# First hidden group by halves of x and units, a hundred small matmuls on zeros at the start, and more matmul groups by halves

## The chip, the cores and the metric

The kernel runs on one core of one Trainium2 chip. The metric is the device time of one execution in microseconds (us); the time before is the median of three runs.

## The reference

Sliding-window causal attention (8 batches, 8 heads, 576 positions, head width 64, window 64), and then a gated feed-forward layer on its output, for 4608 tokens of width 512 with a hidden width of 1536:

```python
scores = scale * np.matmul(q, k.transpose(0, 1, 3, 2))
mask = (rel >= 0) & (rel < window)              # rel = query - key
attn = softmax(np.where(mask, scores, -1e9))
x = np.matmul(attn, v).transpose(0, 2, 1, 3).reshape(B * S, H * D)
gate = np.maximum(x @ w_gate, 0.0)
val = x @ w_val
return (gate * val @ w_out).astype(np.float32)
```

Inputs and output are float32; the kernel computes its products in float16 with float32 sums.

## The kernel before

**Tokens.** The tokens are cut into tiles: tile 0 has 384 tokens, tile 1 has 192, tile 2 has 448, and the others 512. Attention for the first tokens goes by units of 192 tokens (three windows of 64): units 0 and 1 make tile 0, unit 2 makes tile 1. A unit's attention runs through scores (`u_st`, line 277, four row groups of TensorE side by side), exponentials on ScalarE (`u_exp`, L311), masks on VectorE (for units 0 and 1 a bias product on TensorE instead, `bias_mm`, L244), values (`u_pv`, L348, four column groups side by side), reciprocals of the row sums (`u_recip`, L362), the norm on VectorE (`u_norm`, L369) or ScalarE (`u_norm_act`, L381, six instructions), and a transpose on VectorE (`u_turn`, L391). `hh` is 0 or 1, one half of the heads, which is one half of the 512 channels of x: `u_turn(u, (0,))` gives the channel chunks 0 and 1 of unit u's columns of `xt`, and `u_turn(u, (1,))` the chunks 2 and 3.

**Feed-forward of the first tiles.** The hidden features go in slices of 128 (f, 12 of them; "feature 2" is such a slice), each computed as four matmuls over the four channel chunks c. `first_hidden` does blocks 0 to 3 of tile 0: all products with w_gate (RELU on ScalarE, L677), then all with w_val (product with the gate on VectorE, L683 or L686). It packs the work into four blocks, numbered n, one PSUM bank each: block 0 in bank 0 holds features 0 and 1 of unit 0, bank 1 feature 2 of units 0 and 1, bank 2 feature 3 of both units, and bank 3 features 0 and 1 of unit 1. `STEPS` lists, for w_gate and for w_val, in which order (n, chunks cs, units of the bank us, ends) the products go; the weights' first half (`a` = 0) serves chunks 0 and 1, the second half chunks 2 and 3. Then `hidden(0, ...)` does features 4 to 11 in groups of four (L634); `halves` says how many of a group's first features are done by halves: first chunks 0 and 1 of all of them, then chunks 2 and 3. `hidden(1, ...)` does tile 1, and `output(0, ...)` multiplies the hidden values of tiles 0 and 1 with w_out (`out_mm`, L1145): four groups of 128 tokens, features 0 to 3 of all four groups first, then 4 to 7, then 8 to 11. There, features from `OUT_SPLIT` on (but the last) are done as two matmuls of 256 columns rather than one of 512. All later tiles go through seven-product block multiplications (`fast_hidden` L740, `SevenOut` L966), which the change does not touch.

**Order.** The engines' queues are written in an order fixed by hand: `tc.manual_schedule()` and a small planner, `Weaver`. `W.at(t, fn)` puts work of the other engines at a planned time; `W.clock` counts planned TensorE time; `W.advance` records what is due. What a change of the TensorE order does to the clock can thus move other work between two TensorE instructions. Banks are taken in turn (`one_bank`: banks 0 to 3; `two_banks`: 4 to 7). In the first group, the banks 0 to 3 have just held the values of units 0 (banks 0 and 1) and 1 (banks 2 and 3).

**Weights.** GpSimd issues the weights' transfers (`w_load`, L160 and L162), in the order w_gate 0 to 3, w_val 0 to 3, w_gate 4 to 7, w_val 4 to 7, values of v, w_gate 8 to 11, w_val 8 to 11, each of w_gate and w_val in two transfers (a = 0 and 1). `w_need` keeps the planner from recording a product ahead of the planned landing of its weights.

**Products on zeros.** `zero32` is a cleared piece of a tile (`wts`) that is filled later. `keep_hot` (L241) and `heat` (L238) multiply with it and change no result; `heat(1, ...)` is one matmul of 512 columns, which stands ahead of `first_hidden`'s products.

Of the kernel before, what the change touches and what calls it, by code (L numbers as in the profile page):

```python
# [10 lines left out]
FP32 = mybir.dt.float32  # L11
FP16 = mybir.dt.float16
# [35 lines left out]
def kernel(  # L48
# [10 lines left out]
    nc = tc.nc  # L59
# [7 lines left out]
    NC = DM // 128  # L67
    NF = DF // 128
    G = 4
    scale = 1.0 / float(D) ** 0.5  # L70
    TT = 2 * U
# [17 lines left out]
    singles = [psum.tile([128, 512], FP32, name=f"bank{i}") for i in range(8)]  # L89
# [9 lines left out]
    us = persist.tile([128, 4, 2, 128 * HF], FP16)  # L99
# [33 lines left out]
    def v_fixed(i, eng):  # L133

        eng.memset(v16s[i][:, :, :, D:VW].bitcast(FP32), ONE_ONE)
        eng.memset(v16s[i][0:64, 0].bitcast(FP32), 0.0)
# [6 lines left out]
    units = {}  # L143
# [3 lines left out]
    def xt_tile(t):  # L147
        if t not in xts:
            xts[t] = x_sb.tile([128, NC, WT], FP16, name="xt")
        return xts[t]  # L150
# [1 line left out]

    w_done = {}

    def w_load(wt, src, f0, f1, landed):

        if wt is not wo:
            ns = slice(128 * f0, 128 * f1)
            for a in range(2):
                nc.gpsimd.dma_start(wt[:, 2 * a:2 * a + 2, ns], src.rearrange("(a p e) n -> a p e n", a=2, e=2)[a, :, :, ns])  # L160
        if wt is wo:
            nc.gpsimd.dma_start(wo[:, f0:f1], src.rearrange("(c p) n -> p c n", p=128)[:, f0:f1])  # L162
        w_done.update(((wt.name, f, a), landed - 1.3 * (1 - a)) for f in range(f0, f1) for a in range(2))

    def w_need(wt, f, a=1):
        while (wt.name, f, a) not in w_done:
            W.pop()
        W.advance(w_done[wt.name, f, a])
# [7 lines left out]
    def qk_load(b, name, hh):  # L176

        tile_ = nat[b, name, hh] = nats[:, 2 * "kq".index(name) + hh]
        src = (q if name == "q" else k)[b, G * hh:G * hh + G]
        nc.gpsimd.dma_start(tile_, src.rearrange("h (i j) d -> (h i) (j d)", i=32))  # L180
# [54 lines left out]
    def heat(n, to, start=True):  # L235

        for _ in range(n):
            nc.tensor.matmul(to, zero[:, 0:128], zero[:, 0:to.shape[1]], start=start, stop=start, skip_group_check=not start)  # L238
# [9 lines left out]
    def one_bank():  # L248
        taken["one"] += 1
        to = singles[(taken["one"] - 1) % 4]  # L250
        while id(to) in unread:
            W.pop()
        return to
# [9 lines left out]
    def st_tiles(u):  # L263
        d = units.setdefault(u, {})
        if u == 0:
            d["st"] = [one_bank() for _ in range(G)]
        else:
            halves = [two_banks() for _ in range(2)]
            d["st"] = halves[0] + halves[1]
        part_written(d["st"])  # L270
        d["p"] = [None] * G
# [57 lines left out]
    def u_pv(u, hhs=(0, 1), banks=None):  # L329

        d = units[u]
        if "pv" not in d:
            if u >= 6:
                d["pv"] = [bank() for _ in range(2)]
                unread.update(map(id, d["pv"]))
            elif banks:
                d["pv"] = [one_bank() for _ in range(2)]
            else:
                d["pv"] = two_banks()
            part_written(d["pv"])  # L340
        for hh in hhs:
            to = d["pv"][hh]
            for w in range(UB):
                b, vw = divmod(UB * u + w, NG)
                for s in range(2):
                    for j in range(G):
                        c = VW * (2 * w + s)
                        nc.tensor.matmul(  # L348
                            to[32 * j:32 * j + 32, c:c + D + 1], p_of(u, G * hh + j, w)[:, 32 * s:32 * s + 32],
                            v16s[b % 2][:, vw, G * hh + j, 0:D + 1],  # L350
                            start=True, stop=True, skip_group_check=True)
        return 0.27 * len(hhs)
# [66 lines left out]
    def part_written(banks):  # L419
        written.update((id(to), 0) for to in banks)  # L420
# [225 lines left out]
    def first_hidden():  # L646

        g_sb, done = gs[0] = g_sb_p.tile([128, NF, WT], FP16, name="g_sb"), {}
        xt = xt_tile(0)
        r2s = [f_sb.tile([128, 2, WT], FP32, name="pr", bufs=4) for _ in range(2)]  # L650
        r_sbs = [r2s[n // 2][:, n % 2, 0:TT] for n in range(4)]
        blocks = (((0, 0), (1, 0)), ((2, 0), (2, 1)), ((3, 0), (3, 1)), ((0, 1), (1, 1)))
        parts = lambda tile: tile.rearrange("p (w n) -> p w n", w=2)
        STEPS = (
            ((0, (0, 1), (0, 1), False), (0, (2, 3), (0, 1), True), (1, (0, 1), (0, 1), False), (2, (0, 1), (0, 1), False), (1, (2, 3), (0, 1), True), (2, (2, 3), (0, 1), True), (3, (0, 1, 2, 3), (0, 1), True)),
            ((0, (0, 1), (0, 1), False), (2, (0, 1), (0, 1), False), (0, (2, 3), (0, 1), True), (2, (2, 3), (0, 1), True), (3, (0, 1, 2, 3), (0, 1), True), (1, (0, 1, 2, 3), (0, 1), True)),
        )

        def products(h, i, n, cs, us=(0, 1), more=False):
            wt = (wg, wv)[i]  # L660
            block = blocks[n]
            W.advance(W.clock)
            w_need(wt, block[-1][0], cs[-1] // 2)
            whole = i == 0 and n in (1, 2)
            for c in cs if whole else ():
                f = block[0][0]
                nc.tensor.matmul(h[:, 0:TT], wt[:, c, f * 128:f * 128 + 128], xt[:, c, 0:TT],  # L667
                                 start=(c == 0), stop=(c == NC - 1), skip_group_check=True)
            for m in () if whole else us:
                f, u = block[m]  # L670
                for c in cs:
                    nc.tensor.matmul(h[:, U * m:U * m + U], wt[:, c, f * 128:f * 128 + 128], xt[:, c, U * u:U * u + U],  # L672
                                     start=(c == 0 and m == us[0] and not more), stop=(c == NC - 1), skip_group_check=True)
            W.clock += len(us) * len(cs) * (U + 7) / 2400.0

        def relu(n, h):
            nc.scalar.activation(r_sbs[n], h[:, 0:TT], ACT.Relu)  # L677

        def gate(n, h):
            (f, u), (f1, u1) = blocks[n]  # L680
            if f == f1:
                to = g_sb[:, f:f + 1, 0:TT]
                nc.vector.tensor_tensor(to, r_sbs[n].rearrange("p (w n) -> p w n", w=1), h[:, 0:TT].rearrange("p (w n) -> p w n", w=1), MUL)  # L683
                done[f] = TT
            else:
                nc.vector.tensor_tensor(g_sb[:, f:f + 2, U * u:U * u + U], parts(r_sbs[n]), parts(h[:, 0:TT]), MUL)  # L686
                done.update({f: U * u + U, f1: U * u + U})

        for i, then in enumerate((relu, gate)):
            hs = {}  # L690
            for n, cs, us, ends in STEPS[i]:
                more = n in hs
                if not more:
                    hs[n] = one_bank()
                    part_written([hs[n]])
                products(hs[n], i, n, cs, us, more and 0 not in us)
                if ends:
                    W.at(W.clock, lambda n=n, h=hs[n], then=then: then(n, h))
# [186 lines left out]
    wts = persist.tile([128, 4, HF, QN], FP16)  # L885
# [296 lines left out]

    LAST = len(widths) - 1
    BY_ACT = ()
    SPLIT, OUT_SPLIT = [(i, f) for i in range(2) for f in range(4, NF)], 7
    HALVED = [(4, 0, 'P5')] + [(4, 1, name) for name in ('P1', 'P2', 'P3', 'P4')]
    FAST_OUT = (LAST - 5, LAST - 4, LAST - 3, LAST - 2, LAST - 1, LAST)
    O_SUMS = {2: [(24.0, 2, (1, 1)), (26.0, 0, (0, 1))], 3: [(8.0, 3, (1, 0)), (34.0, 1, 2), (34.1, 3, 0)]}
# [8 lines left out]
    with tc.manual_schedule():  # L1197
# [4 lines left out]
            first_load(name)  # L1202
        for name in "kq":
            qk_load(0, name, 1)
        warm = consts.tile([128, 2], FP32)
        nc.vector.memset(warm, 0.0)
        nc.scalar.activation(warm[:, 1:2], warm[:, 0:1], ACT.Exp)
        for i in range(2):
            v_fixed(i, nc.vector)
        zero32 = wts.rearrange("p a f n -> p (a f n)").bitcast(FP32)[:, 0:384]  # L1210
        nc.vector.memset(zero32, 0.0)
        zero = zero32.bitcast(FP16)
        st_tiles(0)
        bands()
        v_load(0, ((1, 0, 128), (3, 0, 64)))
        v_load(1, ((3, 64, 128), (5, 0, 128)))
        w_load(*G3[0], 15.2)
        w_load(*V3[0], 17.7)
        k_zeros()
        band_bias()  # L1220
# [25 lines left out]
        u_turn(0, (0,))  # L1246
        for hh in range(2):
            u_pv(1, (hh,), True)
        heat(1, units[1]["st"][3])
        for hh in range(2):  # L1250
            u_recip(1, (hh,))
        u_norm_act(1, 1)
# [108 lines left out]

        W.advance(15.3)
        first_hidden()
        hidden(0, ((0, TT),), 4, NF, 4, split=SPLIT, halves={(8, 0): 4, (8, 1): 3})
        hidden(1, ((0, U),), each=4, banks=[0, 1, 4, 5, 2, 3, 0, 1, 2, 3, 0, 1])
        taken["one"] += 2
        output(0, (0, 1, 2, 3), (0, 4, 8, NF))
# [71 lines left out]
```

## Time and profile before

| | us |
|---|---|
| median of 3 runs | 298.24 (298.19 to 298.33) |
| the profiled execution | 298.17 |
| its span | 296.5 |
| around the span | 1.67 |
| TensorE matmul busy | 286.9 (97%) |
| TensorE weight loads busy | 241.8 (82%) |
| VectorE busy | 255.4 (86%) |
| ScalarE busy | 203.5 (69%) |
| GpSimd busy | 190.2 (64%) |
| first TensorE matmul starts | 4.42 |
| first product with w_gate starts | 13.80 |

The span is the time between the first and the last instruction of the profiled execution. "PE" is TensorE's matmuls and "PEld" its weight loads, "DVE" is VectorE, "ACT" ScalarE, "POOL" GpSimd and "SP" SyncE. [...] Times given below as "at 13.57" are us from the start of the span.

### The profile page before, as it was taken

How to read it: one execution, taken by the hardware profiler on the slowest of the kernel's cores; microseconds unless marked ns; L12 is line 12 of the kernel's file. 1: busy time of each engine (PE TensorE's matmuls, PEld its weight loads, DVE VectorE, ACT ScalarE, POOL GpSimd, SP SyncE). 2: the span in 40 equal slices, each digit the busy share in tenths (PEclk: the TensorE clock that was granted, in tenths of full speed). 3: DMA queues.
4: the chain of work that ended last, by engine and by line, in shares of the span. 5: the costliest groups of instructions: out<-in, count | busy, mean ns of one | idle time of the engine just before them, and what ended most of it. 6: DMA issues, size and time to landing. Idle time of an engine off the chain costs nothing.

```text
span 296.5 us, 11064 instructions
## 1 busy us (share of the span) xinstructions
PE 286.9 (97%) x4659; PEld 241.8 (82%) x4659; DVE 255.4 (86%) x513; ACT 203.5 (69%) x409; POOL 190.2 (64%) x217
## 2 busy tenths in 40 slices
PE   4799999999999999999999999999999999999995
PEld 2489966996588657998888888888888888888894
DVE  5988989888889799999999999999858985896585
ACT  3744367888288849983897489857985798538860
POOL 8767667898918628476948594859275617441751
PEclk9999999999999999999999999999999999999999
DMA  7999999987998689911599149913911210021013
GB/s 217 185 197 202 195 194 200 237 102 145 156 211 160 103 140 168 212 51 38 85 219 120 42 69 219 127 48 70 172 24 38 75 38 0 3 95 51 1 39 106
DMA packets 62610, 35.22 MB, mean 119 GB/s; under 512 B 39648, under 2 KB 56672, under 8 KB 62560
## 3 DMA queue, kind: packets, MB, share of 16 engines
q0 software_dynamic: 49376, 20.26, 57.9%
q1 hardware_dynamic: 12752, 13.93, 15.2%
q8 instruction: 36, 0.59, 0.8%
q10 hardware_dynamic: 432, 0.33, 0.3%
q14 instruction: 14, 0.11, 0.1%
HBM read 37.75 MB, written 9.44 MB: 159 GB/s over the span
## 4 chain that ended last, share of the span: by engine, by line
PE 94%; DVE 3%; DMA 1%; ACT 0%; issue 0%; DVEq 0%
PE bank L740 49%; PE bank L966 19%; PE bank L874 7%; PE bank L634 6%; PE bank L277 4%; PE bank L1145 4%; PE bank L493 3%; DMA vs<-in_k_dram 1%; PE bank L672 1%; DVE qT L200 1%; DVE kT L200 1%; PE bank L348 1%; PE bank L667 0%; PE bank L241 0%; ACT nats L193 0%; DVE pr L1133 0%
## 5 line engine op out<-in xcount | busy, mean ns | idle before, releaser
L765 POOL TENSOR_TENSOR g_sb<-pr 128x512 f16<-128x512 f32 (+1 forms) x36 | 46.3, 1288 | 50.0 <-ACT pr L782 46.5
L776 DVE TENSOR_TENSOR pr<-bank,pr 128x512 f32<-128x512 f32 (+1 forms) x96 | 60.8, 673 | 4.1 <-ACT pr L759 2.2
L759 ACT COPY pr<-bank 128x512 f32<-128x512 f32 (+1 forms) x96 | 51.1, 588 | 13.8 <-PE bank L740 13.4
L765 DVE TENSOR_TENSOR g_sb<-r,bank 128x512 f16<-128x512 f32 (+1 forms) x48 | 32.4, 676 | 20.1 <-ACT r L809 18.0
L966 PEld LDWEIGHTS <-g_sb 128*128 128x128 f16 x444 | 41.8, 98 | 5.0
L740 PE MATMUL bank<-xc,us 128*128 128x256 f16 (+2 forms) x292 | 42.7, 269 | 0.0
L740 PE MATMUL bank<-xc,vs 128*128 128x256 f16 (+2 forms) x292 | 42.7, 269 | 0.0
L206 POOL DMA_DIRECT2D v<-in_v_dram x41 | 36.8, 1114 | 6.9 <-DMA nats<-in_q_dram 1.5
L740 PEld LDWEIGHTS <-vs 128*128 128x128 f16 x392 | 37.7, 98 | 3.8
L740 PEld LDWEIGHTS <-us 128*128 128x128 f16 x392 | 37.6, 98 | 3.7
L782 ACT ACTIVATE pr<-pr 128x512 f32<-128x512 f32 (+1 forms) x48 | 30.3, 632 | 8.4 <-DVE pr L776 8.4
L450 ACT ACTIVATE pw<-bank 128x512 f16<-128x512 f32 x60 | 32.0, 606 | 2.0 <-PE bank L277 1.6
L809 ACT ACTIVATE r<-bank 128x512 f32<-128x512 f32 (+1 forms) x48 | 28.8, 600 | 5.1 <-PE bank L740 4.1
L740 PEld LDWEIGHTS <-wg 128*128 128x128 f16 x300 | 28.4, 98 | 3.1
L740 PEld LDWEIGHTS <-wv 128*128 128x128 f16 x300 | 28.4, 98 | 2.7
L740 PE MATMUL bank<-xt,wg 128*128 128x256 f16 (+2 forms) x200 | 28.5, 267 | 0.0
L740 PE MATMUL bank<-xt,wv 128*128 128x256 f16 (+2 forms) x200 | 28.5, 267 | 0.0
L916 POOL TENSOR_TENSOR g_sb<-g_sb,xus 128x512 f16<-128x512 f16 x24 | 27.1, 1147 | 0.0
L966 PE MATMUL bank<-wo,g_sb 128*128 128x256 f16 (+1 forms) x222 | 26.6, 270 | 0.0
L749 ACT COPY bank<-bank 128x512 f32<-128x512 f32 (+1 forms) x48 | 25.6, 576 | 0.0
L966 PE MATMUL bank<-wts,g_sb 128*128 128x256 f16 (+1 forms) x222 | 25.6, 270 | 0.0
L459 DVE TENSOR_TENSOR pw<-pw,mask 128x512 f16<-128x512 f16 x60 | 23.2, 429 | 2.2 <-ACT pw L450 1.7
(125 smaller groups left out, 519.5 us busy)
## 6 DMA issues: line engine op xcount, KB each, us to landing
out_dram<-o_sb SPq DMA_DIRECT2D x31, 256.0 KB, 4.0
nats<-in_k_dram POOLq DMA_DIRECT2D x15, 288.0 KB, 5.9
nats<-in_q_dram POOLq DMA_DIRECT2D x15, 288.0 KB, 7.0
v<-in_v_dram POOLq DMA_DIRECT2D x31, 128.0 KB, 8.6
v<-v SPq DMA_DIRECT2D x12, 132.0 KB, 3.4
v<-v SPq DMA_DIRECT2D x24, 66.0 KB, 2.6
wg<-in_moe_w_gate_dram POOLq DMA_DIRECT2D x6, 256.0 KB, 6.8
wv<-in_moe_w_val_dram POOLq DMA_DIRECT2D x6, 256.0 KB, 8.4
```

The lines of the kernel that those rows point to most:

```text
L206: nc.gpsimd.dma_start(v16s[b % 2][lo:hi, g, :, 0:64], v[b, :, 64 * g - 64 + lo:64 * g - 64 + hi].rearrange("h p d -> p h d"))
L450: nc.scalar.activation(d["p"][g].rearrange("p n c -> p (n c)"), d["st"][g], ACT.Exp, scale=scale)
L459: nc.vector.tensor_tensor(d["p"][g], d["p"][g], mask[:, None, :].to_broadcast([128, 2 * QW, 64]), MUL)
L740: nc.tensor.matmul(to[:, HT * m + lo:HT * m + lo + step], w[:, k, 128 * m:128 * m + 128], x[:, k, lo:lo + step], start=(first and m == 0 a ...
L749: nc.scalar.copy(at[j, "B", i][:, 0:TW], at[j, "A", i][:, 0:TW])
L759: nc.scalar.copy(pr[:, i], at[j, "A", i][:, 0:TW])
L765: eng.tensor_tensor(gh[:, f:f + 2, h], pair(r), pair(v), MUL)
L776: nc.vector.tensor_tensor(pr[:, i], to[:, 0:TW], pr[:, i], ADD)
L782: nc.scalar.activation(pr[:, 0], pr[:, 0], ACT.Relu)
L809: nc.scalar.activation(r, to[:, 0:TW], ACT.Relu)
L916: eng.tensor_tensor(to, x, y, op)
L966: nc.tensor.matmul(at[key][:, QN * m * whole:QN * m * whole + n1 - n0], A[:, 128 * m:128 * m + 128], B[:, c, n0:n1] if len(B.shape) == 3 e ...
```

## The change

It has five parts. (1) `STEPS` has a new order for w_gate: eight matmuls on unit 0's first channels (banks 0, 1, 2), then one heating matmul (the entry `None`), then eight on unit 0's second channels, and then unit 1, with bank 3 by halves too; the products of 384 columns (`whole`) are gone, and the heating matmul that stood ahead of the group with them. For w_val, three banks' first halves go first, and bank 1 is last and whole as before. (2) The clearing of `zero32` becomes VectorE's first instruction, and 100 matmuls of 32 x 64 on it, over four column groups in turn, become TensorE's first work. (3) `halves` gets the groups of features 4 to 7: their first two features go by halves. (4) `OUT_SPLIT` goes from 7 to 2. (5) `w_load` gets an argument `parts`, whose default is the old behaviour and which no call gives.

In the recorded queues, ScalarE, GpSimd and SyncE have the same instructions in the same order. On VectorE the clearing stands first, and one mask product of unit 2 passes one gate product (L609). On TensorE, beside the parts named, the 48 value products of unit 2 stand behind the first four matmuls of features 8 to 11 instead of ahead of them.

```diff
-    def w_load(wt, src, f0, f1, landed):
+    def w_load(wt, src, f0, f1, landed, parts=(1, 1)):
...
-            ns = slice(128 * f0, 128 * f1)
-            for a in range(2):
+            for a, n, m in ((a, n, parts[a]) for a in range(2) for n in range(parts[a])):
+                ns = slice(128 * f0 + 512 // m * n, 128 * f0 + 512 // m * (n + 1))
...
         STEPS = (
-            ((0, (0, 1), (0, 1), False), (0, (2, 3), (0, 1), True), (1, (0, 1), (0, 1), False), (2, (0, 1), (0, 1), False), (1, (2, 3), (0, 1), True), (2, (2, 3), (0, 1), True), (3, (0, 1, 2, 3), (0, 1), True)),
-            ((0, (0, 1), (0, 1), False), (2, (0, 1), (0, 1), False), (0, (2, 3), (0, 1), True), (2, (2, 3), (0, 1), True), (3, (0, 1, 2, 3), (0, 1), True), (1, (0, 1, 2, 3), (0, 1), True)),
+            ((0, (0, 1), (0, 1), False), (1, (0, 1), (0,), False), (2, (0, 1), (0,), False), None,
+             (0, (2, 3), (0, 1), True), (1, (2, 3), (0,), False), (2, (2, 3), (0,), False),
+             (1, (0, 1), (1,), False), (2, (0, 1), (1,), False), (3, (0, 1), (0, 1), False),
+             (1, (2, 3), (1,), True), (2, (2, 3), (1,), True), (3, (2, 3), (0, 1), True)),
+            ((0, (0, 1), (0, 1), False), (2, (0, 1), (0, 1), False), (3, (0, 1), (0, 1), False), (0, (2, 3), (0, 1), True), (2, (2, 3), (0, 1), True), (3, (2, 3), (0, 1), True), (1, (0, 1, 2, 3), (0, 1), True)),
         )
...
-            whole = i == 0 and n in (1, 2)
-            for c in cs if whole else ():
-                f = block[0][0]
-                nc.tensor.matmul(h[:, 0:TT], wt[:, c, f * 128:f * 128 + 128], xt[:, c, 0:TT],
-                                 start=(c == 0), stop=(c == NC - 1), skip_group_check=True)
-            for m in () if whole else us:
+            for m in us:
...
+                if step is None:
+                    heat(1, singles[7])
+                    continue
...
-    SPLIT, OUT_SPLIT = [(i, f) for i in range(2) for f in range(4, NF)], 7
+    SPLIT, OUT_SPLIT = [(i, f) for i in range(2) for f in range(4, NF)], 2
...
+        zero32 = wts.rearrange("p a f n -> p (a f n)").bitcast(FP32)[:, 0:384]
+        nc.vector.memset(zero32, 0.0)
+        zero = zero32.bitcast(FP16)
+        for i in range(100):
+            nc.tensor.matmul(singles[7][32 * (i % 4):32 * (i % 4) + 32, 0:64], zero[:, 0:32], zero[:, 0:64], start=True, stop=True, skip_group_check=True)
         warm = consts.tile([128, 2], FP32)
...
-        zero32 = wts.rearrange("p a f n -> p (a f n)").bitcast(FP32)[:, 0:384]
-        nc.vector.memset(zero32, 0.0)
-        zero = zero32.bitcast(FP16)
...
-        heat(1, units[1]["st"][3])
...
-        hidden(0, ((0, TT),), 4, NF, 4, split=SPLIT, halves={(8, 0): 4, (8, 1): 3})
+        hidden(0, ((0, TT),), 4, NF, 4, split=SPLIT, halves={(4, 0): 2, (4, 1): 2, (8, 0): 4, (8, 1): 3})
```

More of the change, by code (lines that the diff above doesn't have):

```diff
@@ L690, in first_hidden @@
             hs = {}
-            for n, cs, us, ends in STEPS[i]:
+            for step in STEPS[i]:
+                if step is None:
+                    heat(1, singles[7])
+                    continue
+                n, cs, us, ends = step
                 more = n in hs
```

## The prediction

> **What bounds the kernel now.** I read the page first, for its chain of work that ended last:
>
> ```profile
> PE 94%; DVE 3%; DMA 1%; ACT 0%; issue 0%; DVEq 0%
> ```
>
> TensorE alone carries 94% of the span, so the question is where the other 6% lie. The waits of PE between 13 and 60 us hold one row, and between 60 us and the end none:
>
> ```profile
> PE bank L672 <- DVE xt L391: 0.7, 1, 0.7
> ```
>
> So after its last stop PE issues without a gap to the end, and whatever ends that stop earlier moves everything behind it. The timeline of PE shows the front (start, busy us, instructions, in brackets the idle time before):
>
> ```profile
> 4.42 2.72 PE L244 MATMUL bank<-bias,ident 128*128 128x384 f16 x8 [4.42 <-DVE bias L130]
> 6.93 1.43 PE L241 MATMUL bank<-wts 128*128 128x384 f32 x2
> 8.35 0.55 PE L277 MATMUL bank<-qT,kT 32*128 32x64 f16 x48
> ...
> 13.09 0.56 PE L348 MATMUL bank<-v,p 128*32 128x65 f16 x48
> 13.57 0.39 PE L238 MATMUL bank<-wts 128*128 128x512 f16 x1
> 13.80 0.49 PE L672 MATMUL bank<-xt,wg 128*128 128x192 f16 x4
> 15.03 0.49 PE L672 MATMUL bank<-xt,wg 128*128 128x192 f16 x4 [0.74 <-DVE xt L391]
> 15.49 1.47 PE L667 MATMUL bank<-xt,wg 128*128 128x384 f16 x8
> 16.80 0.82 PE L672 MATMUL bank<-xt,wg 128*128 128x192 f16 x8
> 17.46 2.80 PE L672 MATMUL bank<-xt,wv 128*128 128x192 f16 x32
> 20.10 2.14 PE L634 MATMUL bank<-xt,wg 128*128 128x192 f16 x24
> ```
>
> A matmul's busy time runs on past the start of the next, so I take costs from starts. 17.46 to 20.10 is 32 matmuls of 192 columns, 0.0825 us each. 15.49 to 16.80 is 8 of 384, 0.164 each. The four at 15.03 need 0.33, so 15.49 comes 0.13 late: a second, hidden wait, for the next transpose. Who ends both is in the timelines of VectorE and ScalarE:
>
> ```profile
> 13.98 0.52 DVE L369 TENSOR_TENSOR xus<-bank,r 128x384 f16<-128x384 f32 x1
> 14.41 1.64 DVE L391 STREAM_TRANSPOSE xt<-xus 128x384 f16<-128x384 f16 x3
> ```
>
> ```profile
> 12.71 2.72 ACT L381 ACTIVATE xus<-bank,r 128x64 f16<-128x64 f32 x12
> ```
>
> The three transposes end at about 14.98, 15.44 and 16.05 (unit 0's second half of channels, then unit 1's two halves), and PE follows each 0.05 later. Before 8.35 PE waits as well: the chain has VectorE's casts and transposes from 5.39 to 10.47, not PE.
>
> **The change, part by part.**
>
> *First group.* Before 15.03 only unit 0's first channels exist, and the old order has four matmuls for them. The new one has eight: blocks 0, 1 and 2. They write banks 0, 1 and 2, which the attention values have just left. Bank 1 is read by the first six of the twelve ScalarE rows, to 14.05; bank 2 by the VectorE row at 13.98, to 14.50. With the heating matmul before them gone, block 0 runs 13.57 to 13.90, block 1 waits to 14.10 and ends at 14.27, block 2 waits to 14.55 and ends at 14.71. The heating matmul, now behind them, takes 0.22 (13.57 to 13.80 in the rows) and ends at 14.93, 0.10 before the transpose lets PE go on at 15.03. That wait itself does not move: its transpose hangs on VectorE's queue, which is the same up to there (and the weights for what follows it land at 14.6, so they would be next, not much earlier).
> Behind 15.03 the old order had 4 of 192, the 0.13, 8 of 384, 8 of 192: 0.33 + 0.13 + 1.31 + 0.66 = 2.43, to 17.46. The new has 24 of 192, ordered so that unit 1's first matmul comes after eight of them, at 15.69 (its transpose: 15.44), and its second channels at 16.35 (16.05). So 24 x 0.0825 = 1.98, to 17.01: **0.45 us earlier**. The split of 384 into two of 192 is within that sum (8 x 0.001).
>
> *What could be late next.* ScalarE's four RELUs free the banks for w_val; they come 0.39 apart, the second at about 16.72, so bank 2 is free by 17.6 and wanted at 17.67; cover 0.07. The w_val steps put three blocks' first halves ahead of the second halves, so w_val's second half is wanted at 18.0 as before. The weights are the transfers that PE now meets 0.45 earlier; issue and landing, one row of the DMA issues for each window around one issue:
>
> ```profile
> wg<-in_moe_w_gate_dram POOLq DMA_DIRECT2D x1, 256.0 KB, 7.1
> ```
>
> ```profile
> wg<-in_moe_w_gate_dram POOLq DMA_DIRECT2D x1, 256.0 KB, 8.7
> ```
>
> The first is w_gate features 4 to 7, second half: issued 12.95, landed 20.07. PE enters that group at 19.65; feature by feature it would want it at 19.98 and stall 0.1. The new grouping (first halves of two features together) wants it at 20.31: no stall, and that is what those two entries are worth. The w_val one delays nothing (landed 23.05, wanted 23.5). The second row is features 8 to 11, first half: issued 16.70, landed 25.35 to 25.4. Here the recorded order moves: the 48 value products of unit 2 now come behind four of these matmuls, not before them, so they are wanted at 25.51 and no longer at 26.56; cover 0.1, and the smallest left. w_out's first third lands at 39.66 (29.46 + 10.2; wanted 40.03), its second at 43.9 (wanted 44.1). On VectorE only one mask product passes one gate product. I price all this at 0, with up to 0.2 in the range.
>
> *Output by halves.* 5 features x 4 row groups: 20 matmuls of 512 become 40 of 256. In rows of one form, 13 of 512 take 2.98 us, the last 0.38 in all: 0.217 each; 8 of 256 take 1.04, the last 0.27: 0.110 each. 20 x (0.220 - 0.217) = **+0.05** (0 to 0.1), all on PE's path.
>
> *Hundred small matmuls.* They start when VectorE's memset, now its first (0.38 us from 0.89), is done: 1.3. Bias products can start at 4.42 at the earliest, since they wait for VectorE. The nearest row is L348, same 32-column weights, 65 columns wide: 13.09 to 13.57 is 48, 10 ns each, four side by side. But the clock is low there in the front: 4.42 to 6.93 is 8 of 384 columns, 0.314 each against 0.164 later (the page's granted clock reads 1.00 all the same). So 20 ns each, 2 us, over at 3.3. The upper bound takes no two side by side: 64/384 of 0.314 is 52 ns, 5.2 us, over at 6.5. I take 2 us, free behind the 4.42. What they may buy is a warm clock under the bias products: 8 x 0.15 = 1.2 us of PE, none of it on the chain, because 8.35 is set by VectorE. **0**. VectorE's reordered memsets end at 2.7 as before and it then idles 1.48: 0. The new argument of the weight load is passed by no call: 0.
>
> *Sum.* -0.45 + 0.05 = -0.40. The profiled execution is 296.5 of span and 1.67 around it, 298.17, 0.07 under the median of 298.24. From the median: 297.84.
>
> **The rivals.**
> *Weights become the wait.* PE runs into features 8 to 11, or w_out, and stands there. For it: cover of 0.1 to 0.2 where there was 0.5 and more. Against: each landing would have to be late by more than that, and transfers in this stretch are issued by POOL without regard to PE. Price: 0.1 to 0.4 given back, 297.95 to 298.25.
> *A faster front.* If the early clock also shortened the chain to 13.57, the gain passes 0.6. Against: the attention products at 8.35 and 10.51 both take 0.55, so the clock was up at 8.35 already. It would take 0.2 us from a chain in which PE's own part is some 2 us: 297.4 to 297.6.
> *Small matmuls outlast the front (slower).* If each costs e ns, they end at 1.3 + 0.1e. By then the clock is up, so bias and keep-hot products take 8 x 0.164 + 0.85 = 2.2, and scores start at 3.5 + 0.1e instead of 8.35. ScalarE has 0.46 us of slack between the two halves of its exponentials; the rest lands on the end. So the loss is 0.1e - 5.3: it begins at e = 53, just past the upper bound above, uses up the gain at 57, and makes 298.8 at 63 and 300.5 at 80. Against: 10 ns in the row at 13.09. For: these would be the first instructions of the queue, a place of which the trace has no row.
> [...]
> *It does not do it.* If block 2's bank came free 0.1 later, the heating matmul would push past 15.03 by as much; it costs 0.1 for each 0.1, down to no gain, 298.2.
>
> **How the numbers follow.** Forecast 0.66 (297.7 to 297.95); weights or the bank 0.14; faster front 0.11; slower 0.09. A measurement of this kernel tells about 0.2%, 0.6 us, from no change. The forecast and the second case lie within it, as do small ends of the others: same 0.78, faster 0.13, slower 0.09. The range takes the faster front down to 297.5 and the weights up, with a little of the slower case, to 298.35.
>
> **What would show it.** In the changed profile: eight products from 13.57, the only PE wait still ending at 15.03 on L391 but under 0.2 long; w_val starting at 17.01 and features 4 to 7 at 19.65; no PE wait behind; the small matmuls over before 4.42 and scores still at 8.35; every later stage earlier by 0.4. It is wrong if 15.03 moves, if a weight load waits at 25.4, or if bias products start after 4.42.

## The result, and the profile after

| | before | after |
|---|---|---|
| median, us | 298.3 (298.19 to 298.98, 12 runs) | 299.88 (299.42 to 302.36, 12 runs) |
| profiled execution, us | 298.17 | 299.65 |
| its span, us | 296.5 | 297.9 |

The ratio of the mean times is 1.0066, with a 95% interval of 1.0046 to 1.0085 (that of the medians is 1.0053). The changed kernel is slower by 0.66%, where a gain of 0.4 us had been forecast.

The timeline of PE in the changed kernel, up to the second pass of features 4 to 7 (start, busy us, instructions, in brackets the idle time before):

```profile
1.40 1.52 PE L1211 MATMUL bank<-wts 128*32 128x64 f16 x100 [1.40 <-DVE warm L1213]
4.40 2.72 PE L244 MATMUL bank<-bias,ident 128*128 128x384 f16 x8 [1.48 <-DVE bias L130]
...
9.05 0.55 PE L277 MATMUL bank<-qT,kT 32*128 32x64 f16 x48 [0.69 <-DVE qT L200]
...
14.28 1.30 PE L670 MATMUL bank<-xt,wg 128*128 128x192 f16 x8
15.42 0.38 PE L238 MATMUL bank<-wts 128*128 128x512 f16 x1
15.74 2.14 PE L670 MATMUL bank<-xt,wg 128*128 128x192 f16 x24
17.71 1.48 PE L670 MATMUL bank<-xt,wv 128*128 128x192 f16 x16
```

The hundred small matmuls are over at 2.92, and the first group runs without a wait: from the first scores (L277) to the first product with w_val it takes 17.71 - 9.05 = 8.66 us, where it took 17.46 - 8.35 = 9.11. That is the gain of 0.45 that was forecast. But the scores themselves start 0.70 later. Among the waits of PE over the whole span, two rows name what else is new (us in total, times, longest):

```profile
PE bank L1147 <- issue: 0.6, 1, 0.6
...
PE bank L634 <- DVE g_sb L609: 0.2, 1, 0.2
```

Both are later than the first group, where the kernel before had no wait at all. Placed in the timeline of PE:

```profile
23.59 2.80 PE L634 MATMUL bank<-xt,wv 128*128 128x192 f16 x32
26.61 0.49 PE L634 MATMUL bank<-xt,wg 128*128 128x192 f16 x4 [0.22 <-DVE g_sb L609]
...
47.92 4.54 PE L1147 MATMUL bank<-wo,g_sb 128*128 128x256 f16 x38
53.03 1.25 PE L1147 MATMUL bank<-wo,g_sb 128*128 128x512 f16 x8 [0.57 <-issue]
```

The span's change is then made up as follows, each from starts on PE (the 0.05 is what is left of the output stage without the stop):

| stage | change, us |
|---|---|
| front, to the first scores (8.35 to 9.05) | +0.70 |
| first group (9.11 to 8.66) | -0.45 |
| w_val of features 4 to 7 to w_val of features 8 to 11 (5.87 to 6.25) | +0.38 |
| forty half-size output products | +0.05 |
| the stop at 53.03 | +0.74 |
| sum | +1.42 (span: 297.9 - 296.5 = 1.4) |

The stop stands at 0.57 in the timeline, because idle time is counted from a matmul's end; between starts the gap is 0.84, of which a product takes 0.11. "issue" says that PE waited for nothing that the profile shows. What stands ahead of the stop in time is among the trace's transfers, on a queue that the page calls "instruction" (packets, MB, share):

```profile
q8 instruction: 37, 0.61, 0.8%
```

The kernel before has this row for it:

```profile
q8 instruction: 36, 0.59, 0.8%
```

0.61 MB in 37 packets is 16 KB each, and one takes 0.88 to 1.6 us. TensorE has 9582 instructions in the changed kernel (4787 matmuls, as many weight loads, and eight of its sequencer) and 9326 before, exactly 256 fewer, and one packet fewer. Of the sixteen kernels profiled here, those with up to 9382 instructions have 36 packets and those with 9442 and more have 37. From these counts I take 256 instructions to a packet: an estimate, since no record says what a packet holds. Counting TensorE's instructions from one in order of their starts, number 1986 is the one that starts late at 53.03. It is 194 + 7 x 256. Below, a block is the 256 instructions from such a number on, and its packet the one as far along in the order of packets, the first with the block at 450; that pairing is mine too. From 15 us on, and leaving out the waits for a tensor that the matmul itself reads or for a bank that it writes, the sixteen kernels have 21 stops of 0.41 to 2.83 us from start to start. **Each of the 21 stands at 194 plus a multiple of 256**, and each ended 1.20 to 1.55 us after the end of a packet. The packet here ran from 50.52 to 51.48, 1.55 us ahead of 53.03; it began 3.5 us after the block before had begun to run (46.98).

The same look at the kernel before shows what the forecast had missed: its instruction 450 = 194 + 256 is the first of the eight last products of w_gate, it starts at 16.80, and the packet ends at 15.22, 1.58 us ahead. The stops ended 1.20 to 1.55 us behind theirs, so by these distances, an estimate, the first group already ran with hardly any cover, 0.03 to 0.38 us.

### The profile page after: what moved, and what is told of

Same layout as the page of the kernel before. It is cut to its first block, busy times and chain, and to the rows that moved or that the text cites. A ratio compares the mean times of both kernels' runs of the same rounds, so it can differ in the third digit from the quotient of the medians.

```text
span 297.9 us, 11320 instructions
## 1 busy us (share of the span) xinstructions
PE 289.0 (97%) x4787; PEld 245.7 (82%) x4787; DVE 256.0 (86%) x513; ACT 203.0 (68%) x409; POOL 189.7 (64%) x217
## 4 chain that ended last, share of the span: by engine, by line
PE 93%; DVE 4%; DMA 1%; issue 0%; ACT 0%; DVEq 0%
PE bank L742 49%; PE bank L968 19%; PE bank L876 7%; PE bank L634 5%; PE bank L1147 4%; PE bank L277 4%; PE bank L493 3%; PE bank L670 2%; DMA vs<-in_k_dram 1%; DVE p L318 1%; DVE qT L200 1%; DVE kT L200 1%; PE bank L348 1%; DVE nats L193 0%; PE bank L241 0%
```

## The experiments

I first ran the parts alone, then moved the blocks, then took parts away from the changed kernel one by one. "Before" had medians of 298.35 to 298.4 in these runs.

**The four parts alone.** Only the new orders (part 1):

```diff
-            ((0, (0, 1), (0, 1), False), (0, (2, 3), (0, 1), True), ...
+            ((0, (0, 1), (0, 1), False), (1, (0, 1), (0,), False), (2, (0, 1), (0,), False), None, ...
```

> Before, with the new order of the first hidden group alone (heating matmul behind the eight products, no other part). Both theories say that this part does what the prediction said: products with w_val start 0.45 us earlier than before, scores still at 8.35, no new wait; span about 296.05 and 297.85 us, with a granted clock of 1.0. If the lower clock of some executions of the changed kernel comes from the heating matmul's new place, some executions here show it too (mean clock 0.992 to 0.998) and are 0.5 to 3 us longer.

298.79, ratio 1.0012 (1.0 to 1.0023): no gain. The timeline of PE shows why:

```profile
13.56 1.30 PE L670 MATMUL bank<-xt,wg 128*128 128x192 f16 x8
14.70 0.38 PE L238 MATMUL bank<-wts 128*128 128x512 f16 x1
15.02 0.82 PE L670 MATMUL bank<-xt,wg 128*128 128x192 f16 x8
16.75 1.48 PE L670 MATMUL bank<-xt,wg 128*128 128x192 f16 x16 [0.92 <-DVE us L561]
```

The eight early products and 15.02 are as forecast, but after eight of the 24 products PE stands until 16.75 (a stop of 1.08, the 0.08 of the product before it not counted), and w_val starts at 18.07. The releaser named (L561 writes `us`, which the first group does not read) is only the event nearest in time: the instruction at 16.75 is number 450, and its packet ran from 14.48.

Only the clearing and the hundred small matmuls (part 2):

```diff
+        for i in range(100):
+            nc.tensor.matmul(singles[7][32 * (i % 4):32 * (i % 4) + 32, 0:64], zero[:, 0:32], zero[:, 0:64], ...
```

> Before, with the clearing first and the 100 small matmuls alone. Theory 1 (each part has a cost of its own): the small matmuls cost something in the front or in the clock: the first load of k lands at 5.2 and not at 4.65, scores at 9.05, span 297.1, and some executions have a mean clock of 0.992 to 0.998 with 0.5 to 3 us more. No stall in the output product. Theory 2 (the late load was chance, and the small matmuls hurt only by shifting the instruction stream by 200): scores at 8.35 in most executions, clock 1.0, and any loss is a gap of TensorE without a wait, somewhere in the output product of tile 0 (0.3 to 0.8 us). If they cost nothing: 298.2.

300.47 (six runs), ratio 1.0063 (1.0039 to 1.0088). The scores start at 8.96, so the late front comes with this part. A stop of 0.72 stands at 230.62, instruction 7874 = 194 + 30 x 256.

Only the output by halves (part 4):

```diff
-    SPLIT, OUT_SPLIT = [(i, f) for i in range(2) for f in range(4, NF)], 7
+    SPLIT, OUT_SPLIT = [(i, f) for i in range(2) for f in range(4, NF)], 2
```

> Before, with OUT_SPLIT 2 alone. Theory 1 (TensorE ran out of instructions at 53.03, since half-size products use up instructions twice as fast behind the 112 small value products): there is a gap without a wait in the output product here too, of 0.4 to 2.4 us by where the fetch falls; span 296.9 to 299. Theory 2 (the 200 added instructions put the fetch there): no gap, +0.05 us, 298.3.

300.6 (six runs), ratio 1.0073 (1.0047 to 1.0098), from 20 more matmuls. Its timeline of PE in the output:

```profile
46.81 0.61 PE L493 MATMUL bank<-v,pw 128*32 128x65 f16 x43
47.35 2.14 PE L1145 MATMUL bank<-wo,g_sb 128*128 128x256 f16 x18
50.62 2.56 PE L1145 MATMUL bank<-wo,g_sb 128*128 128x256 f16 x20 [1.13 <-issue]
```

Instruction 1730 stands at 50.62 after a gap of 1.40; a second gap of 1.35, which I had not expected, is at 114.23, instruction 3778. Each of the two blocks before these numbers holds a run of small value products (L493, 112 from 46.24, of which the first row shows the last 43, and 128 from 108.44), 10 ns from start to start. Ahead of 50.62 the half-size products come at 0.11 us each, where a whole one takes 0.22, so that the count runs twice as fast; at 114.23, far behind the changed output, only the count has moved: this place is number 3738 in the kernel before.

Only the groups of features 4 to 7 by halves (part 3):

```diff
-        hidden(0, ((0, TT),), 4, NF, 4, split=SPLIT, halves={(8, 0): 4, (8, 1): 3})
+        hidden(0, ((0, TT),), 4, NF, 4, split=SPLIT, halves={(4, 0): 2, (4, 1): 2, (8, 0): 4, (8, 1): 3})
```

> Before, with the entries (4, 0) and (4, 1) of halves alone. Theory 1 (recording the four mask products of unit 2 ahead of the first gate product makes TensorE wait for bank 0 at the first product of features 8 to 11): a wait of 0.1 to 0.4 us on L609 near 26, span 296.6 to 296.9, 298.3 to 298.6. Theory 2 (that wait appears only because TensorE came 0.45 us earlier relative to the weights and copies): no wait, 298.2.

298.56, ratio 1.0 (0.9988 to 1.0011): no difference shown. The four mask products of unit 2 stand ahead of the first gate product here too, but PE has no wait on L609: from w_val of features 4 to 7 to w_val of features 8 to 11 it takes 29.70 - 23.83 = 5.87, as before. Theory 2 held.

**Blocks of instructions put to the test.** Sixteen small matmuls (32 instructions) put into idle time of the kernel before, behind the first `keep_hot` product:

```diff
+        for i in range(16):
+            nc.tensor.matmul(singles[7][32 * (i % 4):32 * (i % 4) + 32, 384:448], zero[:, 0:32], zero[:, 0:64], ...
```

> Before, with 16 of the same small matmuls on zeros put behind the first keep-hot product, where TensorE waits for scores until 8.35 anyway; nothing else changes. Theory F (TensorE's instructions come in blocks of 256; the block that begins at its 450th matmul-or-weight-load row is fetched only when the block before it is begun, near 10.7, and is usable at about 16.7; more rows ahead of a fixed point of the program bring that point nearer to the end of what is loaded): scores stay at 8.35, but TensorE stops without a wait at the 450th row, now 16 products earlier in the program, until about 16.7; the first product with w_val starts at 18.9 to 19.2 instead of 17.46 and the span is 1.3 to 1.8 us longer, 297.8 to 298.3 (time 299.5 to 300). Theory Z (what the small matmuls cost, they cost in the front by themselves): no gap, at most 0.1 us, 298.3.

304.5 (four runs), ratio 1.0207 (1.0181 to 1.0233), worse than expected. Timeline of PE:

```profile
13.66 0.39 PE L238 MATMUL bank<-wts 128*128 128x512 f16 x1
16.50 1.44 PE L672 MATMUL bank<-xt,wg 128*128 128x192 f16 x8 [2.45 <-DVE us L561]
17.73 2.43 PE L667 MATMUL bank<-xt,wg 128*128 128x384 f16 x8
```

Number 450 is now the first product with w_gate, and it starts at 16.50, where number 450 ran at 16.80 in the kernel before, so that nearly the whole group lies behind it. After the stop 8 matmuls of 384 columns take 2.27 from start to start, 1.31 before (this execution's mean granted clock is 0.994), and two more stops follow, 0.62 and 1.53 at numbers 1730 and 3778. The scores start at 8.67, 0.32 late. All of that is in the loss of 6 us.

The new orders with eight instructions fewer ahead of the group (the heating matmul out, three float32 products made single float16 ones):

```diff
-        keep_hot(units[1]["st"][3][:, 0:2 * U])
+        heat(1, units[1]["st"][3][:, 0:2 * U], False)
```

> The new first group alone, with 8 rows fewer ahead of it: its own heating matmul is left out and the three float32 keep-hot products are single float16 ones (they change no result). Theory F: the 450th row lies 4 products later in the program, so the 1.08 us gap that the new group alone showed at 16.75 becomes about 0.75, and the span 296.7 to 296.8 (298.4 to 298.5); if the float32 products count as one row pair in the stream, 0.16 to 0.25 instead of 0.33 is saved. Rival (the gap at 16.75 is a wait for VectorE's us products, as the waits have it): gap unchanged at 0.9 to 1.1.

The stop moved four products on, still ending at 16.77, and is 0.83 long now, counted the same way (0.75 expected); w_val started at 17.76, 0.31 earlier than in the run with the new orders alone. The waits name "issue" for it this time, no longer L561. The span stayed at 297.1, at a mean granted clock of 0.994 in this execution. The median is 298.69, ratio 1.0012 (1.0002 to 1.0021).

**One part taken away from the changed kernel.** Without the small matmuls (`for i in range(100)` and its body out):

> The changed kernel without the 100 small matmuls (the clearing stays first). Theory F: scores back at 8.35, but without the 200 rows the 450th row falls into the first group again: a gap of about 1.0 us without a wait near 16.7, and a second one of 0.5 to 2 us behind the 112 value products, where the block that begins at row 1730 is due at about 49; span 297.8 to 299.5, 299.5 to 301. Theory Z (the small matmuls are what costs): no gap near 16.7, span 296.5 to 297.0, 298.2 to 298.7.

302.02 (four runs), ratio 1.0141 (1.01 to 1.0181): 2 us slower than with them. The scores are at 8.34 again, but numbers 450, 1730 and 3778 stop PE, by 1.17, 1.69 and 2.02 us from start to start. In the changed kernel the 200 added instructions move all these places, and one stop of 0.74 is left.

Without the output by halves (`OUT_SPLIT` back at 7):

> The changed kernel with OUT_SPLIT back at 7 (40 rows fewer between 41 and 54 us). Theory F: no gap at 53; front late by 0.6 as in both kernels with the small matmuls, first group 0.45 better, 0.3 to 0.4 lost near 26.6 where the first product of features 8 to 11 waits for a gate product behind four masks: span 296.9 to 297.2, 298.6 to 298.9. Rival (the gap at 53 belongs to something else, a late transfer): gap stays, 299.5.

300.9 (299.14 to 304.27, eight runs), ratio 1.009 (1.0048 to 1.0132). No stop at 53, but one of 0.44 at number 7874, and in the profiled execution, at a mean granted clock of 0.993, the second group of scores takes 0.83 us and not 0.55. The loss at the first product of features 8 to 11, which I had expected to stay, is gone (5.87). No gain over the changed kernel is shown.

Without the two new entries of `halves`:

> The changed kernel without the entries (4, 0) and (4, 1) in halves. Theory M (these entries and the earlier products make the order fixed by hand put four mask products ahead of the gate product that frees bank 0, which costs 0.38 us at 26.61): if the entries are the cause, the wait at 26.61 is gone and the span is 297.5; a wait for the weights of features 4 to 7 of at most 0.1 may come at about 20.7. If the earlier products alone shift the order, the wait stays and the span is 297.9. The stop at 53 stays in both.

299.66, ratio 1.0058 (1.0033 to 1.0083). Timeline of PE:

```profile
23.75 2.80 PE L634 MATMUL bank<-xt,wv 128*128 128x192 f16 x32
26.48 0.56 PE L348 MATMUL bank<-v,p 128*32 128x65 f16 x48
26.97 2.81 PE L634 MATMUL bank<-xt,wg 128*128 128x192 f16 x32
29.62 2.80 PE L634 MATMUL bank<-xt,wv 128*128 128x192 f16 x32
```

The wait is gone: from w_val to w_val 29.62 - 23.75 = 5.87, as before, where the changed kernel has 6.25. But the entries alone do not bring it: it is missing in the run with them alone (above), and in the changed kernel without small matmuls, without the output by halves and with 112 small matmuls the stage takes 5.87 too, with 30 it takes 5.92, though all of these have the entries. With 92 it is there (6.26). The timelines of VectorE and of GpSimd in the changed kernel:

```profile
23.56 2.54 DVE L318 TENSOR_TENSOR p<-p,mask 128x384 f16<-128x384 f16 x4 [0.71 <-ACT p L311]
26.02 1.94 DVE L609 TENSOR_TENSOR g_sb<-pr,bank 128x384 f16<-128x384 f32 x4
```

```profile
23.90 1.72 POOL L216 COPY v<-v 64x512 f16<-64x512 f16 x2 [2.88 <-DMA v<-in_v_dram]
```

The same with the entries alone:

```profile
23.80 2.08 DVE L318 TENSOR_TENSOR p<-p,mask 128x384 f16<-128x384 f16 x4 [0.86 <-ACT p L311]
25.81 1.94 DVE L609 TENSOR_TENSOR g_sb<-pr,bank 128x384 f16<-128x384 f32 x4
```

```profile
23.42 1.72 POOL L216 COPY v<-v 64x512 f16<-64x512 f16 x2 [2.50 <-DMA v<-in_v_dram]
```

All four mask products of unit 2 run ahead of the first gate product, which frees the bank that the matmul at 26.61 writes. They are not of one length: 0.36, 0.77, 1.19 and 0.35 in the changed kernel, the two long ones begun during GpSimd's two copies of v (L216). In the sixteen profiles all 23 mask products of this unit that begin well inside these copies take 0.43 to 1.19, and the 38 others 0.34 to 0.36. In the changed kernel the copies end at 25.61, and the gate product starts 2.43 after PE's w_val (23.59); with the entries alone the copies come earlier, end at 25.14, and it starts 1.98 after (23.83). So the 0.38 needs both, the order of VectorE and masks stretched during the copies. Stretched masks cost without the entries too: the run with small matmuls alone takes 6.09 for this stage and the first trimmed one 6.16, with three masks ahead of the gate product. In the kernel before the gate product runs ahead of the fourth mask product:

```profile
24.65 0.54 DVE L609 TENSOR_TENSOR g_sb<-pr,bank 128x384 f16<-128x384 f32 x1
25.12 0.72 DVE L318 TENSOR_TENSOR p<-p,mask 128x384 f16<-128x384 f16 x1
```

Taking the entries out saved no time in total: the front came at 9.22 in that execution, and PE was idle for 0.9 at 53.10 (1.14 from start to start).

**The number of small matmuls.** 92 and 112 instead of 100 move all blocks by 16 and 24 instructions, and the bias products behind them start at 4.40 and 4.41:

```diff
-        for i in range(100):
+        for i in range(92):
```

> The changed kernel with 92 small matmuls on zeros instead of 100. Theory F (TensorE's instructions come in blocks of 256, counted over matmuls and weight loads, and a block that is begun too early finds nothing): 16 instructions fewer put the block that begins at 53.03 eight output products later, where about 53.2 is wanted and the block is there at about 52.8. So the stop of 0.74 at 53.03 is gone, no other comes, and the profiled span is 0.7 shorter than that of the changed kernel, 297.2 (median about 299.1). Theory P (the stop belongs to the place, the output products by halves): stop stays, span 297.9.

> The changed kernel with 112 small matmuls on zeros instead of 100. Theory F: 24 instructions more put the block's beginning on instruction 1962 of the changed kernel, which runs at 50.88 there; the block is asked for at most 0.1 us earlier, so it is there at about 52.9, and the stop is 1.8 to 2.0 us at about 51 instead of 0.74 at 53.03: span 298.9 to 299.2, median about 301. The twelve matmuls themselves cost nothing, since TensorE waits to 4.40 behind them. Theory P: span 297.9.

With 92 the output runs through, in the timeline of PE:

```profile
48.65 5.62 PE L1147 MATMUL bank<-wo,g_sb 128*128 128x256 f16 x46
54.11 0.55 PE L742 MATMUL bank<-xt,wg 128*128 128x224 f16 x4
```

All 46 products follow each other, and no other stop appears. The span was 297.9 all the same, since the profiled execution ran its attention products slower (0.83 us a group of scores, not 0.55; the mean granted clock is 0.998) and reached w_val at 18.44 instead of 17.71. The median is 299.41 (298.66 to 303.04). The fastest run is 0.76 under the fastest of the changed kernel (299.42), but the fastest without the entries of `halves` (298.87) and with 112 small matmuls (298.88) lie nearly as low with a stop each, so a saving in time is not shown; that the stop is gone is.

With 112 my expectation failed: instruction 1986 ran at 51.49 without a stop, and its packet began at 49.19, 1.7 us after the block before it was begun and not 3.5. A stop came elsewhere, at number 4034:

```profile
113.32 1.68 PE L876 MATMUL bank<-wo,g_sb 128*128 128x512 f16 x7
115.91 1.24 PE L876 MATMUL bank<-wo,g_sb 128*128 128x512 f16 x5 [0.90 <-issue]
```

There the packet began at 113.73, 4.3 us after the block before it was begun (109.41). So in the sixteen kernels the stops stood at counted places alone, but not at all of them, and at the 21 stops the packet began from 0.9 us ahead of the beginning of the block before to 4.3 us behind it. What sets that is open. The reasons that the theories give, a block that is asked for when the one before it is begun, and finds nothing when it is begun too early, are in no record of a trace; what the runs show is the numbers and the times. Over the sixteen profiles the median is 3.25 us behind for packets begun between 13 and 30 us and 0.15 for those after 200 us; the kernel before moves 204 GB/s in its first 60 us and 55 after 200. The median is 299.81 (298.88 to 302.1).

> The changed kernel with 30 small matmuls on zeros instead of 100. It asks what makes the front late (scores at 9.05 instead of 8.35). Theory E (the early fetch of a second block, at 6.55 in the changed kernel, which 100 matmuls bring forward, disturbs the first loads): with 30 the second block is begun only in the attention products, and the scores start at 8.35 again. Theory Q (any work of TensorE ahead of the loads does it, or the clearing): scores still at 8.9 to 9.1. By theory F the third block would then begin where the first group's products stand (instruction 590 of the changed kernel), so a stop of 2 to 3 us between 13.4 and 16.5 and another of about 1 at 47.5 to 49; span 299 to 300.5.

With 30 small matmuls: 307.9, ratio 1.0315 (1.03 to 1.033). Theory E fell: no packet runs early any more (the first is at 13.30), yet the scores still start at 9.06. As theory F says, number 450 now stops PE inside the value products (0.9 idle at 15.75, where 2 to 3 had been expected); there are six stops in all, 7.05 us from start to start, more than I expected, and behind the one at 118.62 the granted clock is 0.5 for 3.4 us (the execution's mean is 0.994). The waits of PE from 60 us on hold two of the six and no other wait:

```profile
PE bank L277 <- issue: 1.7, 1, 1.7
PE bank L493 <- issue: 1.7, 1, 1.7
```

**What is left of the front, and of the first group.** The kernel before with a single small matmul at the start:

> The kernel before with the clearing first and one single small matmul on zeros as TensorE's first work. In the six runs with small matmuls (30 to 112 of them) one 4.6 KB packet of the first loads, begun at 2.11 to 2.17, took 1.0 to 1.5 us, where the longest took 0.45 to 0.77 in the eight runs without; the first k load then landed at 4.9 to 5.35 instead of 4.5 to 4.65. Theory G (TensorE's first instruction, at 1.40 instead of 4.42, sets off something that occupies one transfer engine for about 0.9 us, the length of a packet of instructions): one matmul is enough; one packet begun at about 2.15 takes over 1.0 us, the k load lands at 4.9 to 5.3 and the scores start at 8.9 to 9.1; span 297.0 to 297.4. Theory H (it is the number of matmuls, or their traffic): k load at 4.5 to 4.65 and scores at 8.35, span 296.5 to 296.8.

298.32, ratio 1.0003 (0.9994 to 1.0012), scores at 8.37: theory G fell too. One is not enough, thirty are.

The new orders with none of the `heat` and `keep_hot` products, 14 instructions fewer than the new orders alone:

> The new order of the first group alone, without its heating matmul and without the three products that keep the clock up. Theory F: six instructions fewer than in the run that had three single matmuls there move the block's beginning three products on, to 15 products after the second stop; it is there at about 16.8 still, so the products with w_val start at 17.5 instead of 17.76, about where they start in the kernel before (17.46): span 296.6 to 296.8. Rival: without those products the clock falls to half in the front, scores or attention values take twice their time, and the span is over 297.5.

298.47, ratio 1.0008 (0.9997 to 1.002), span 296.5. Timeline of PE:

```profile
8.44 0.83 PE L277 MATMUL bank<-qT,kT 32*128 32x64 f16 x48 [1.31 <-DVE qT L200]
...
13.61 4.05 PE L670 MATMUL bank<-xt,wg 128*128 128x192 f16 x32
17.50 2.80 PE L670 MATMUL bank<-xt,wv 128*128 128x192 f16 x32
```

w_val starts at 17.50, as theory F said, although the products before it ran slower (32 in 3.89, 0.122 each and not 0.0825), and number 450 stands at 16.76. In the kernel before and in six variants (the new orders alone, both trimmed ones, the changed kernel without small matmuls, the output alone, one small matmul) number 194 runs between 10.76 and 11.09, and number 450 at 16.75 to 16.80, whatever product it is. In these seven kernels no product of the first group that stands behind number 450 ran before 16.75. The time itself is not fixed: with sixteen added matmuls number 450 runs at 16.50, and with 30 small matmuls at 15.75, its packet beginning 1.7 us after number 194 and not the 3.5 to 3.6 of the seven. None of the fourteen variants is shown to be faster than the kernel before.

## Why the prediction was wrong

*First group, -0.45: right, with luck.* 14.28 is 13.57 + 0.70 + 0.01, and 17.71 is 17.01 + 0.70. But it needed a condition that the working never named: that number 450 stands outside the group. By itself the new order lost the gain in a stop of 1.08 at number 450. The term "24 x 0.0825 = 1.98" is right only because the small matmuls, priced at 0, move that number to 12.10, into the value products, 4.7 us after its packet's end.

*"Hundred small matmuls. ... 0": the step that failed most, with +0.70 in the front and the stop of 0.74 behind it.* Their own time was forecast well: over at 2.92 (3.3 forecast), bias products at 4.40, and 13 ns each ((1.52 - 0.61) / 70 between 100 and 30 of them), where 20 had been taken and the nearest row had 10. "Free behind the 4.42" overlooked that the front hangs on a load. In the timeline of VectorE:

```profile
5.24 0.74 DVE L193 CAST nats<-vs 128x576 f16<-128x576 f32 x1 [0.89 <-DMA vs<-in_k_dram]
6.09 1.25 DVE L200 STREAM_TRANSPOSE kT<-nats 128x576 f32<-128x576 f32 x1
```

The kernel before:

```profile
4.68 0.60 DVE L193 CAST nats<-vs 128x576 f16<-128x576 f32 x1 [0.31 <-DMA vs<-in_k_dram]
5.39 1.25 DVE L200 STREAM_TRANSPOSE kT<-nats 128x576 f32<-128x576 f32 x1
```

The load lands at 5.22 instead of 4.65, and casts, transposes and scores follow it. That is 0.57 of the 0.70; the rest is VectorE's cast, 0.74 and not 0.60. With the small matmuls alone the load is only 0.23 late, and the scores are still 0.61 late, because the second cast takes 0.84 there and not 0.45. What lengthens these casts is open. Of the load's sixteen landings in the trace fifteen had come by 4.57, and the last came 0.65 later. In the seven kernels with 30 or more small matmuls at the start, the last landing is 0.45 to 0.78 behind the fifteenth; in the nine others 0.03 to 0.15. That the matmuls bring it about is shown (with the clearing first but without them the scores start at 8.34); by what way is open, as neither an early packet (none with 30) nor the first instruction (one matmul, scores at 8.37) explains it. I had priced VectorE's clearing and TensorE's idle time, and not the transfers of the same microseconds. And the 200 instructions were not free either way: they move every later block.

*"What they may buy is a warm clock under the bias products": they bought none.* The eight bias products take 2.72 in both kernels. That 0.314 here against 0.164 later is a matter of the clock was my reading of the rows, and that small matmuls ahead make these products faster a guess, which no run shows: 8 x 0.314 in both kernels, with a hundred ahead and with none.

*"Output by halves, +0.05": right for the products, wrong for the part.* The products themselves cost that (the sum as written gives 0.06), but they pass twice as many instructions in the same time (0.11 a product, not 0.22), behind 112 value products, and the stop of 0.74 stands among them. It goes with the count: 92 small matmuls instead of 100 take it away.

*"On VectorE only one mask product passes one gate product ... at 0": wrong by 0.38.* I had seen the exchange and not asked which bank the gate product frees, nor how long the masks take while GpSimd copies v (0.77 and 1.19, not 0.36). PE's next group waits for that bank (0.22 idle before 26.61). In four variants with the same exchange the masks take 1.89 to 2.12 together and not 2.54, the stage takes 5.87, and the exchange costs nothing.

*Weights: not put to the test.* There is no wait for a weight load at 25.4 or anywhere else. But PE enters features 4 to 7 at 20.36 and not at 19.65, and features 8 to 11 at 26.61 and not at 25.51, so the late front gave the cover that had been counted as 0.1.

*The rivals.* The slower one, "small matmuls outlast the front", named the right part and the wrong mechanism; its price began at 53 ns, and they took 13. (Its slack of 0.46 for ScalarE is PE's idle time before the scores at 10.51; ScalarE itself has 0.27 before its second half, at 10.91.) Against my own list of what would show the prediction wrong, one of three came true: 15.03 moved (to 15.74). Of what was to be seen if it were right, the scores at 8.35 and the absence of later waits failed too.

*The median.* Five of the twelve runs of the changed kernel have a mean granted clock of 0.992 to 0.994 and spans of 298.8 to 300.7; the other seven 297.7 to 298.2. In three profiled executions of variants with that mean (without the output by halves, 112 small matmuls, the first trimmed one) the granted clock is 0.5 for one stretch of 3.4 us in the front. With them the median lies 0.23 above the profiled execution. What brings these stretches on is open.

## What to carry to other kernels

Where a stage consists of many short matmuls, count instructions as well as time: here all 21 stops stood 256 matmuls and weight loads, or a multiple of that, behind number 194, a packet began up to 4.3 us after the block before it, took 0.97 in the median, and no block's first instruction ran earlier than 1.2 us after its packet's end. A stop with the releaser "issue", or with one that the waiting instruction doesn't read, is to be looked up by its instruction's number before it is put down to an engine. And filler work is not free because its engine is idle: here it moved the number of everything behind it by 200, and with it a load that the front hangs on landed 0.57 late.

## What the runs showed of the hardware that I had not expected

- The queue "instruction" moved 36 packets of 16 KB in kernels of up to 9382 TensorE instructions and 37 in those of 9442 and more; the 21 stops were all at numbers 194 + 256 n. With sixteen added matmuls of no use the kernel took 6 us longer (304.5), and dropping 14 instructions was worth 0.57 in the first group (18.07 to 17.50).
- Thirty or more small matmuls at 1.40 go with the last of the first load's sixteen landings being 0.45 to 0.78 us behind the fifteenth, in seven kernels of seven (0.03 to 0.15 in the nine others); one matmul doesn't do it.
- VectorE's mask products of 128 x 384 take 0.34 to 0.36 us, and 0.43 to 1.19 when begun during GpSimd's copies of v: 23 of 23 against 38 of 38.
- Small matmuls of 32 x 64 over four column groups start 13 ns apart.
- 1.5 us of them before the bias products made these no faster: 0.314 us for 384 columns in both kernels.
